# Re-ordering the first tiles and the middle matmuls of a linear-attention and routed-MLP kernel

## The chip, the cores and the metric

The kernel runs on one core of a Trainium2 chip. The metric is the device time of one execution in microseconds, the median of several runs. TensorE (PE) multiplies and writes to PSUM, which has eight banks. VectorE (DVE), ScalarE (ACT) and GpSimd (POOL) are the other engines; SyncE (SP) only issues DMAs. Each engine works through its own list of instructions in order and waits for semaphores of the others.

## The reference

With x of 2048 tokens by 640 (bf16) the result is x + A(xn) + B(x), where xn is x normalised over its 640 columns.

A is linear attention with 32 heads of 20: q, k, v = xn · wqkv; phi(t) = (t + 1 if t > 0, else exp(t)) + 1e-6; per head kv = phi(k)ᵀ v and z = sum over tokens of phi(k); the output is phi(q) · kv divided by phi(q) · z, times wo.

B takes the 8 tokens with the largest x · w_r, computes (silu(x w_gate) * (x w_up)) w_down for these, scales it by sigmoid of the score, and adds it, and x itself, to the result.

## The kernel before

The tokens form T = 16 tiles of 128, the 640 columns KC = 5 blocks of 128. The whole program is written out by hand: the order of the calls in the source is the order on each engine.

**Front and loop (L294 to L483).** For each tile t: DVE takes its statistics in two halves and joins them (`ln_stats`, L161, L164, L165); POOL turns the variance into a factor (L167, L170; for tiles 0 and 1 ACT does it, L174, L175); DVE scales the tile (`ln_scale`, L179); PE turns tiles 0 to 4 (`turn_pe`, L191), with copies out by ACT or DVE (L199, L201), and a DMA turns the rest (L204). Then come the k product (`k_mm`, L209), ACT's exp and relu of it (L225, L226), DVE's combination pk (`k_phi`, L232), and the product G of xn and pk, summed over all tiles in five PSUM banks (`g_mm`, L270). Units of the q product (`q_mm`, L243; `q_act`, L255 and L256; `q_phi`, L262) are interleaved, one for each tile. An extra column of the k weights gives the router's score; ACT stores it into r_all (L227). Loads of x are issued by SP; that of tile 3 waits for a small POOL memset (`late_x3`, L146, L147), which stands among POOL's constants. `const_piece` builds other constants on POOL during the loop.

**Middle (L486 to L780).** PE turns r_all (L487), sums pk over the tokens for z (`z_mm`, L498: four products with 32 columns each, side by side in the array, per tile), finishes G, and multiplies the 16 rows of candidates by ones to spread them over all partitions (L515). ACT copies G out of PSUM (L522, L530) and the column sums zs (L526). DVE picks the 8 tokens; POOL gathers their columns into xsT (L563). PE then interleaves: the rest of G (`grest_mm`, L279), denominators (`den_mm`, L578; `spread_mm`, L595), kv by groups of six heads (`kv_mm`, L618; five groups of 120 columns and one of 40), each group masked by DVE (L630, L638) and multiplied by wo to M (`m_mm`, L651; copied out by ACT L663 or DVE L665, and sent to its place M_sb by SP, L666), and the MLP of the 8 tokens: gate and up (`gu_mm`, L672, 32 columns, four side by side), ACT's exp, ln, exp (L724, L729, L731), two DVE products to hm (L737, L738), its turn (L741) and copy hT (L743), the down product (L748) and the add by an indirect DMA (L758).

**End.** The remaining q units, then for each tile the output product (`o_mm`, L789), DVE's add of x (L799) and the store (L806).

Of the kernel before, what the change touches and what calls it, by code (L numbers as in the profile page):

```python
# [17 lines left out]
C = 8  # L18
# [3 lines left out]
HG = 6  # L22
GB = HG * DH
NG = 6
FJ = F // 4
YW = D // 4
EPS_BF16 = 1.0013580322265625e-05
# [9 lines left out]

def group(g):

    return GB * g, min(GB, D - GB * g)  # L40


@with_exitstack
def kernel(
# [49 lines left out]
    ones_r = sb([T, P], BF16, "ones_r")  # L94
    tileoff = sb([P, T, C], F32, "tileoff")
    diag = sb([T, T], F32, "diag")
    oh8 = sb([P, C], F32, "oh8")
# [6 lines left out]
    maskkv = sb([GB, HG, DH], BF16, "maskkv")  # L104
    wr_rows = sb([KC, P], BF16, "wr_rows")
    wrT = sb([P, KC], BF16, "wrT")
    r_all = sb([P, T], BF16, "r_all")
    kvT = sb([GB, NG, GB], BF16, "kvT")
    M_nat5 = sb([GB, D], BF16, "M_nat5")
    spw = sb([P, 2, 4, 256], BF16, "spw")  # L110

# [4 lines left out]
    def psb(b):  # L116
        return ps[:, b, :].bitcast(BF16)
# [14 lines left out]
    make_identity(nc, ident[:])  # L132
    nc.gpsimd.memset(half[:, 0:1], EPS_BF16)
    nc.gpsimd.memset(half[:, 1:2], -0.5)
    nc.gpsimd.memset(gbig[:], 1.0)


# [9 lines left out]
        nc.sync.dma_start(x_sb[:, 3, :], x_v[:, 3, :])  # L147

    gbig_side(True)
    late_x3()  # L150
    gbig_side(False)

    stat = {}

# [156 lines left out]
    warm(4, P)  # L311
    turned(0, 7, "V", 0, 2)
    turned(0, 7, "A", 2, KC)
    ln_stats(2, "a")
    ln_scale(1)
    for kc in range(3):
        for h in range(2):
            k_one(0, 5, kc, h, HW)
# [43 lines left out]
    ln_scale(5)  # L362
    turn_dma(5)
    ln_stats(6)
    ln_stats(7, "a")
    k_phi(3)
    ln_scale(6)
    turn_dma(6)
    ln_stats(7, "b")
    q_mm(0, 7)  # L370
    q_act(0, 7)

    def const_piece(i):
# [22 lines left out]
            )  # L396
        elif i == 4:
            nc.gpsimd.memset(ones_r[:], 1.0)
            nc.gpsimd.memset(diag[:], 0.0)
            nc.gpsimd.affine_select(  # L400
                out=diag[:], in_=diag[:], compare_op=ALU.not_equal, fill=1.0, base=0,
                pattern=[[-1, T]], channel_multiplier=1,
            )
            nc.gpsimd.memset(oh8[:], 0.0)
            for j in range(4):
                nc.gpsimd.affine_select(
                    out=oh8[:], in_=oh8[:], compare_op=ALU.not_equal, fill=1.0,
                    base=-32 * j, pattern=[[-1, C]], channel_multiplier=1,
                )
        elif i == 5:  # L410
            nc.gpsimd.iota(itmp[:], pattern=[[1, P]], base=0, channel_multiplier=0)
            nc.gpsimd.tensor_copy(iot[:], itmp[:])
            nc.gpsimd.iota(
                itmp[:].rearrange("p (t c) -> p t c", c=C), pattern=[[P, T], [0, C]], base=0,
                channel_multiplier=0,
            )
            nc.gpsimd.tensor_copy(
                tileoff[:], itmp[:].rearrange("p (t c) -> p t c", c=C)
            )
        elif i == 6:  # L420
            nc.gpsimd.iota(itmp[:, 0:1], pattern=[[0, 1]], base=4 * S, channel_multiplier=1)
# [12 lines left out]
    def load_wo(h):  # L434
        if h == 0:
            src = A_wo[0 : 5 * GB, :].rearrange("(g e) n -> e g n", e=GB)
            nc.sync.dma_start(wo_sb[:, 0:5, :], src)
        else:
            nc.sync.dma_start(wo_sb[0 : D - 5 * GB, 5, :], A_wo[5 * GB : D, :])

    pieces += [lambda: load_wo(0), lambda: load_wo(1)]
    for kc in range(KC):
# [41 lines left out]


    u = T - 3 - 1  # L486
    nc.tensor.transpose(psb(5)[0:T, 0:P], r_all[:], ident[:])  # L487
# [21 lines left out]
    nc.vector.tensor_tensor(  # L509
        out=candm[:], in0=cand[:].unsqueeze(2).to_broadcast([T, 2, T, C]),  # L510
        in1=diag[:].unsqueeze(1).unsqueeze(3).to_broadcast([T, 2, T, C]), op=ALU.mult,
    )
    q_phi(u)
# [99 lines left out]

    def kv_mm(g0, g1, bank):
        for g in range(g0, g1):
            f0, w = group(g)
            for c in range(KC):
                nc.tensor.matmul(  # L618
                    ps[0:w, bank, (g - g0) * GB : (g - g0) * GB + w],
                    lhsT=wv_sb[:, c, f0 : f0 + w],  # L620
                    rhs=GT[:, c, f0 : f0 + w],
                    start=(g == g0 and c == 0), stop=(c == KC - 1),
                    skip_group_check=True,
                )
# [9 lines left out]
        )  # L634

    def kv_mask5(bank):
        w = group(5)[1]
        nc.vector.tensor_tensor(  # L638
            out=kvT[0:w, 5, 0:w], in0=ps[0:w, bank, GB : GB + w], in1=mask2[0:w, 0:w],
            op=ALU.mult,  # L640
        )

    late = big.tile([P, T * D], BF16, tag="pk", name="late")
# [2 lines left out]
    M_nat = big.tile([P, KC, D], BF16, tag="wk_sb", name="M_nat")  # L646

    def m_mm(g, b):
        w = group(g)[1]
        for h in range(2):  # L650
            nc.tensor.matmul(  # L651
                ps[0:w, b + h, 0:HW],
                lhsT=kvT[0:w, g, 0:w],
                rhs=wo_sb[0:w, g, h * HW : (h + 1) * HW],
                start=True, stop=True,
            )

    def m_out(g, b, by_act=False):
        f0, w = group(g)
        nat = M_nat[0:w, g, :] if g < 5 else M_nat5[0:w, :]  # L660
        dst, src = nat.rearrange("p (b f) -> p b f", b=2), ps[0:w, b : b + 2, 0:HW]
# [4 lines left out]
        nc.sync.dma_start(M_sb[f0 // KC : (f0 + w) // KC, :, :], nat)  # L666


    def gu_mm(w, b):
# [52 lines left out]
    scale_by(0, 0)  # L722
    gu_mm(wg_sb, 7)
    nc.scalar.activation(e1, ps[:, 7, 0:FJ], AF.Exp, scale=-1.0)  # L724
# [12 lines left out]
    nc.vector.tensor_tensor(out=hm, in0=ps[:, 7, 0:FJ], in1=sg, op=ALU.mult)  # L737
    nc.vector.tensor_tensor(out=hm, in0=hm, in1=ps[:, 0, 0:FJ], op=ALU.mult)  # L738
    q_unit(13, 1)
    for j in range(3):  # L740
        nc.tensor.transpose(psb(7)[:, j * P : (j + 1) * P], hm[:, j * P : (j + 1) * P], ident[:])  # L741
# [125 lines left out]
```

## Time and profile before

| | us |
|---|---|
| median of 3 runs | 111.91 (111.89 to 112.18) |
| profiled execution | 112.47 |
| its span | 110.8 |
| PE busy | 104.9 |
| DVE busy | 82.4 |
| ACT busy | 57.8 |
| POOL busy | 29.6 |

The profile is of one execution. The span runs from the first instruction to the last. A row of its timeline has start, length, engine, line, operation, what is written and read, and in brackets how long the engine was idle before and what ended that. The chain of waits follows the work that ended last back to the start; its pieces have start and length and do not overlap. PE's matmuls are pipelined: a row's length holds the time until the result is out, and the next matmul may start before that. PEld is the load of weights into the array.

### The profile page before, as it was taken

The numbers are of one execution on the slowest core, as the hardware profiler recorded it, in microseconds if no ns is written. First come the engines' busy times: TensorE is split into PE (matmuls) and PEld (weight loads), VectorE is DVE, ScalarE is ACT, GpSimd is POOL, SyncE is SP. The second block draws the span as 40 slices with busy tenths as digits, with TensorE's granted clock in tenths as the row PEclk, the third lists the DMA queues.
The fourth block names the chain that finished last, engine by engine and source line by source line (L and its number), as shares of the span: only waits on it lengthen the run. The fifth ranks groups of instructions, "written<-read, shape, count | busy, mean of one in ns | idle before, by whom it ended". The sixth has DMA issues, their size and how long they took to land.

```text
span 110.8 us, 2414 instructions
## 1 busy us (share of the span) xinstructions
PE 104.9 (95%) x881; PEld 65.0 (59%) x881; DVE 82.4 (74%) x182; ACT 57.8 (52%) x121; POOL 29.6 (27%) x83
## 2 busy tenths in 40 slices
PE   5979999999999999999999999999999999999980
PEld 2346565555556555566556578954656667777760
DVE  0767988878888898998798892586586669966680
ACT  1538746853875568555875583867599330000000
POOL 7406023537855588740000002200330000000000
PEclk9999999999999999999999999999999999999998
DMA  3999930241799999999955799415225927894333
GB/s 84 312 297 340 382 130 8 52 90 31 164 273 219 183 194 361 310 357 341 352 212 189 215 291 373 133 57 171 74 15 162 339 99 175 280 345 149 124 121 116
DMA packets 23011, 22.49 MB, mean 203 GB/s; under 512 B 8791, under 2 KB 21719, under 8 KB 22999
## 3 DMA queue, kind: packets, MB, share of 16 engines
q1 hardware_dynamic: 21021, 20.27, 63.6%
q10 hardware_dynamic: 1834, 2.02, 5.3%
q0 software_dynamic: 144, 0.04, 0.5%
q8 instruction: 7, 0.11, 0.4%
q14 instruction: 5, 0.04, 0.1%
HBM read 14.42 MB, written 5.28 MB: 178 GB/s over the span
## 4 chain that ended last, share of the span: by engine, by line
PE 77%; DVE 7%; DMA 5%; POOL 3%; issue 2%; ACT 2%; SPq 1%; DVEq 0%; POOLq 0%
PE ps L789 19%; PE ps L243 17%; PE ps L209 15%; PE ps L270 12%; DMA x_sb<-in_A_x_dram 5%; PE ps L279 4%; DVE xn L179 2%; POOL rs L170 2%; PE ps L618 2%; PE ps L651 2%; PE ps L672 2%; DVE st L164 1%; DVE xn L799 1%; PE ps L578 1%; PE ps L498 1%
## 5 line engine op out<-in xcount | busy, mean ns | idle before, releaser
L209 PE MATMUL ps<-wk_sb,xnT 128*128 128x320 bf16 (+1 forms) x160 | 25.2, 300 | 0.4 <-DVE xnT L201 0.3
L243 PE MATMUL ps<-xnT,wq_sb 128*128 128x512 bf16 x100 | 24.2, 379 | 0.0
L789 PE MATMUL ps<-late,pqT 128*128 128x320 bf16 (+2 forms) x165 | 22.3, 295 | 0.0
L209 PEld LDWEIGHTS <-xnT 128*128 128x128 bf16 x160 | 15.3, 98 | 9.2 <-DVE xnT L201 0.8
L270 PE MATMUL ps<-pk,xn 128*128 128x512 bf16 x80 | 19.9, 379 | 0.3 <-DVE pk L232 0.3
L225 ACT ACTIVATE ek<-ps 128x640 bf16<-128x640 f32 x16 | 11.3, 704 | 15.9 <-PE ps L209 15.9
L789 PEld LDWEIGHTS <-pqT 128*128 128x128 bf16 x165 | 15.8, 98 | 6.3 <-issue 0.2
L799 DVE TENSOR_TENSOR xn<-ps,x_sb 128x640 bf16<-128x640 f32 (+3 forms) x18 | 13.2, 747 | 5.5 <-PE ps L789 5.5
L262 DVE SCALAR_TENSOR_TENSOR pqT<-eq,rq 128x512 bf16<-128x512 bf16 x20 | 13.7, 684 | 3.5 <-ACT rq L256 3.5
L243 PEld LDWEIGHTS <-wq_sb 128*128 128x128 bf16 x100 | 11.5, 118 | 8.0 <-issue 0.3
L232 DVE SCALAR_TENSOR_TENSOR pk<-ek,rk 128x640 bf16<-128x640 bf16 x16 | 12.9, 804 | 1.7 <-ACT rk L226 1.7
L255 ACT ACTIVATE eq<-ps 128x512 bf16<-128x512 f32 x20 | 12.3, 617 | 2.7 <-PE ps L243 2.7
L270 PEld LDWEIGHTS <-xn 128*128 128x128 bf16 x80 | 7.6, 98 | 9.0 <-issue 0.6
L256 ACT ACTIVATE rq<-ps 128x512 bf16<-128x512 f32 x20 | 12.3, 616 | 0.0
L170 POOL TENSOR_TENSOR rs<-rs,half 128x1 f32<-128x1 f32 x14 | 11.2, 801 | 1.1
L167 POOL TENSOR_TENSOR rs<-mv,half 128x1 f32<-128x1 f32 x14 | 6.3, 447 | 18.5 <-DVE mv L165 18.5
L226 ACT ACTIVATE rk<-ps 128x640 bf16<-128x640 f32 x16 | 11.2, 700 | 0.0
L161 DVE BATCH_NORM_STATS2 st<-x_sb 128x6 f32<-128x320 bf16 x16 | 7.6, 476 | 3.9 <-DMA x_sb<-in_A_x_dram 3.9
L179 DVE TENSOR_SCALAR xn<-x_sb,mv,rs 128x640 bf16<-128x640 bf16 x16 | 7.1, 445 | 4.5 <-POOL rs L170 4.2
L164 DVE BATCH_NORM_STATS2 st<-x_sb 128x6 f32<-128x320 bf16 x16 | 7.6, 478 | 0.0
L563 POOL COPY xsT<-xnT 128x5 bf16 x8 | 1.7, 207 | 21.7 <-DVE junk L693 18.3
L185 DVE TENSOR_TENSOR x_sb<-x_sb,xn 128x640 bf16<-128x640 bf16 x16 | 6.9, 474 | 0.0
(121 smaller groups left out, 91.1 us busy)
## 6 DMA issues: line engine op xcount, KB each, us to landing
x_sb<-in_A_x_dram SPq DMA_DIRECT2D x6, 320.0 KB, 7.4
wg_sb<-in_B_w_gate_dram SPq DMA_DIRECT2D x5, 384.0 KB, 4.3
wu_sb<-in_B_w_up_dram SPq DMA_DIRECT2D x5, 384.0 KB, 5.1
wd_sb<-in_B_w_down_dram SPq DMA_DIRECT2D x3, 640.0 KB, 7.7
xxd<-x_sb SPq DMA_DIRECT2D x2, 640.0 KB
out_dram<-xn SPq DMA_DIRECT2D x8, 160.0 KB, 1.8
x_sb<-xxd SPq DMA_DIRECT2D x2, 640.0 KB, 4.9
out_dram<-xn ACTq DMA_DIRECT2D x7, 160.0 KB, 3.3
```

Source lines behind the costliest of these rows:

```text
L170: nc.gpsimd.tensor_tensor(out=rs[:, 1:2], in0=rs[:, 0:1], in1=half[:, 1:2], op=ALU.pow)
L209: nc.tensor.matmul(ps[:, b + h, 0:w], lhsT=xnT[:, kc, t * P : (t + 1) * P], rhs=wk_sb[:, kc, h * HW : h * HW + w], start=(kc == 0), stop=( ...
L225: nc.scalar.activation(e[:], ps[:, b : b + 2, 0:HW], AF.Exp)
L226: nc.scalar.activation(r[:], ps[:, b : b + 2, 0:HW], AF.Relu)
L232: nc.vector.scalar_tensor_tensor(out=pk[:, t, :].rearrange("p (b f) -> p b f", b=2), in0=e[:], scalar=1.0, in1=r[:], op0=ALU.min, op1=ALU.add,
L243: nc.tensor.matmul(ps[:, b, :], lhsT=wq_sb[:, kc, :].rearrange("p (f m) -> p m f", m=KC)[:, m, :], rhs=xnT[:, kc, tb * TBLK : (tb + 1) * T ...
L255: nc.scalar.activation(e[:], ps[:, b, :], AF.Exp)
L256: nc.scalar.activation(r[:], ps[:, b, :], AF.Relu)
L262: nc.vector.scalar_tensor_tensor(out=pqT[:, m, tb * TBLK : (tb + 1) * TBLK], in0=e[:], scalar=1.0, in1=r[:], op0=ALU.min, op1=ALU.add,)
L270: nc.tensor.matmul(ps[:, c, :], lhsT=xn[:, t, c * P : (c + 1) * P], rhs=pk[:, t, 0:512], start=(t == 0), stop=(t == T - 1),)
L789: nc.tensor.matmul(ps[:, b, 0 : c1 - c0], lhsT=pqT[:, kc, t * P : (t + 1) * P], rhs=M_sb[:, kc, c0:c1], start=(kc == 0), stop=(kc == KC - 1),)
L799: nc.vector.tensor_tensor(out=xn[:, t, c0:c1].rearrange("p (b f) -> p b f", f=w), in0=ps[:, b : b + n, 0:w], in1=x_sb[:, t, c0:c1].rearran ...
```

## The change

**Front.** DVE scales tile 1 ahead of the first half of tile 2's statistics. Tile 7's statistics are taken in one piece, ahead of tile 3's pk. POOL clears r_all ahead of its constants, and the memset that releases the load of tile 3 comes behind both selections of gbig instead of between them.

On DVE, first tiles 1 and 2 (st, mv, rs and the digit: statistics, their aggregate and the factor of that tile). Before:

```order
L201 COPY xnT_77<-ps_109 128x2x128
L161 BN_STATS st2_184<-x_sb_75 128x6
L179 TENSOR_SCALAR xn_76<-x_sb_75,mv1_158,rs1_159 128x640
L164 BN_STATS st2_184<-x_sb_75 128x6
L165 BN_AGGR mv2_185<-st2_184 128x2
```

Now:

```order
L205 COPY xnT_77<-ps_110 128x2x128
L183 TENSOR_SCALAR xn_76<-x_sb_75,mv1_160,rs1_161 128x640
L165 BN_STATS st2_187<-x_sb_75 128x6
L168 BN_STATS st2_187<-x_sb_75 128x6
L169 BN_AGGR mv2_188<-st2_187 128x2
```

Tile 1's scaling has moved up by one place. Then, on DVE, tiles 6 and 7. Before:

```order
L165 BN_AGGR mv6_335<-st6_334 128x2
L161 BN_STATS st7_342<-x_sb_75 128x6
L232 SCALAR_TENSOR_TENSOR pk_79<-ek3_327,rk3_328 128x640
L179 TENSOR_SCALAR xn_76<-x_sb_75,mv6_335,rs6_336 128x640
L164 BN_STATS st7_342<-x_sb_75 128x6
L165 BN_AGGR mv7_343<-st7_342 128x2
L262 SCALAR_TENSOR_TENSOR pqT_78<-eq0_358,rq0_359 128x512
L179 TENSOR_SCALAR xn_76<-x_sb_75,mv7_343,rs7_344 128x640
```

Now:

```order
L169 BN_AGGR mv6_337<-st6_336 128x2
L165 BN_STATS st7_344<-x_sb_75 128x6
L168 BN_STATS st7_344<-x_sb_75 128x6
L169 BN_AGGR mv7_345<-st7_344 128x2
L236 SCALAR_TENSOR_TENSOR pk_79<-ek3_329,rk3_330 128x640
L183 TENSOR_SCALAR xn_76<-x_sb_75,mv6_337,rs6_338 128x640
L266 SCALAR_TENSOR_TENSOR pqT_78<-eq0_360,rq0_361 128x512
L183 TENSOR_SCALAR xn_76<-x_sb_75,mv7_345,rs7_346 128x640
```

The second half and the aggregate of tile 7 have moved ahead of tile 3's pk and tile 6's scaling.

**Middle.** The column sums of tile 15 join the run of the others; ACT copies zs ahead of G. r_all has 128 columns, candm and ones_r 128 rows (the added ones are zero), so that both products use the whole array. The last kv group takes the last 120 columns: its product has 120 rows, its 80 columns that group 4 has already are zero in kvT, and only its last 40 rows of M are sent. The up product follows the gate product at once, then kv groups 4 and 5, q unit 13, M's groups 4 and 5, the turn of hm, and three matmuls of q unit 14 where there were two. `scale_by(0, 2)` comes after q unit 13's phi.

On PE, around the last kv groups and M. Before, between the gate products and the last three matmuls of q unit 13, with the up products in the place of the dots:

```order
L618 MATMUL ps<-GT,wv_sb 40x40
L672 LDWEIGHTS xsT
L672 MATMUL ps<-wu_sb,xsT 32x384
...
L651 MATMUL ps<-wo_sb,kvT 120x320
L651 LDWEIGHTS kvT
L651 MATMUL ps<-wo_sb,kvT 40x320
...
L243 LDWEIGHTS wq_sb
L243 MATMUL ps<-xnT,wq_sb 128x512
```

Now, with the rest of the last kv group and of q unit 13 in the place of the dots:

```order
L672 MATMUL ps<-wu_sb,xsT 32x384
L620 LDWEIGHTS wv_sb
L620 MATMUL ps<-GT,wv_sb 120x120
...
L620 MATMUL ps<-GT,wv_sb 120x40
L247 LDWEIGHTS wq_sb
L247 MATMUL ps<-xnT,wq_sb 128x512
...
L651 LDWEIGHTS kvT
L651 MATMUL ps<-wo_sb,kvT 120x320
L740 LDWEIGHTS late
L740 MATMUL ps<-ident,late 128x128
```

The up products have gone ahead of the kv groups, M's two groups behind q unit 13, and no output of 40 rows is left. The diff, cut to its core:

```diff
+W0 = NG * GB - D
 def group(g):
-    return GB * g, min(GB, D - GB * g)
+    return min(GB * g, D - GB)
...
-    r_all = sb([P, T], BF16, "r_all")
+    r_all = sb([P, P], BF16, "r_all")
...
+    nc.gpsimd.memset(r_all[:], 0.0)
     nc.gpsimd.memset(gbig[:], 1.0)
...
     gbig_side(True)
+    gbig_side(False)
     late_x3()
-    gbig_side(False)
...
+    ln_scale(1)
     ln_stats(2, "a")
-    ln_scale(1)
...
     ln_stats(6)
-    ln_stats(7, "a")
+    ln_stats(7)
     k_phi(3)
     ln_scale(6)
     turn_dma(6)
-    ln_stats(7, "b")
...
             nc.gpsimd.memset(ones_r[:], 1.0)
+            nc.gpsimd.memset(candm[:], 0.0)
+            nc.gpsimd.memset(kvT[:, NG - 1, 0 : W0], 0.0)
...
-            nc.sync.dma_start(wo_sb[0 : D - 5 * GB, 5, :], A_wo[5 * GB : D, :])
+            nc.sync.dma_start(wo_sb[:, 5, :], A_wo[D - GB : D, :])
...
-    nc.tensor.transpose(psb(5)[0:T, 0:P], r_all[:], ident[:])
+    nc.tensor.transpose(psb(5)[:, 0:P], r_all[:], ident[:])
...
-    for t in range(T - 1):
+    for t in range(T):
         z_mm(t)
...
     g_mm(T - 1, 3, KC)
-    z_mm(T - 1)
-    for c in range(4):
-        nc.scalar.copy(GT[:, c, 0:512], ps[:, c, :])
...
-    nc.scalar.copy(GT[:, 4, 0:512], ps[:, 4, :])
+    for c in range(KC):
+        nc.scalar.copy(GT[:, c, 0:512], ps[:, c, :])
...
-            f0, w = group(g)
+            f0, c0 = group(g), (W0 if g == NG - 1 else 0)
             for c in range(KC):
                 nc.tensor.matmul(
-                    ps[0:w, bank, (g - g0) * GB : (g - g0) * GB + w],
-                    lhsT=wv_sb[:, c, f0 : f0 + w],
-                    rhs=GT[:, c, f0 : f0 + w],
+                    ps[0:GB, bank, (g - g0) * GB : (g - g0 + 1) * GB - c0],
+                    lhsT=wv_sb[:, c, f0 : f0 + GB],
+                    rhs=GT[:, c, f0 + c0 : f0 + GB],
...
     nc.scalar.activation(e1, ps[:, 7, 0:FJ], AF.Exp, scale=-1.0)
+    gu_mm(wu_sb, 0)
     kv_mm(4, 6, 6)
     scale_by(0, 1)
+    nc.scalar.activation(e1, e1, AF.Ln, bias=1.0)
+    nc.scalar.activation(sg, e1, AF.Exp, scale=-1.0)
     kv_mask(4, 5, 6)
     kv_mask5(6)
-    nc.scalar.activation(e1, e1, AF.Ln, bias=1.0)
-    gu_mm(wu_sb, 0)
-    nc.scalar.activation(sg, e1, AF.Exp, scale=-1.0)
+    nc.vector.tensor_tensor(out=hm, in0=ps[:, 7, 0:FJ], in1=sg, op=ALU.mult)
+    nc.vector.tensor_tensor(out=hm, in0=hm, in1=ps[:, 0, 0:FJ], op=ALU.mult)
+    q_unit(13, 1)
     m_mm(4, 2)
     m_out(4, 2, True)
     m_mm(5, 4)
     m_out(5, 4, True)
-    scale_by(0, 2)
-    nc.vector.tensor_tensor(out=hm, in0=ps[:, 7, 0:FJ], in1=sg, op=ALU.mult)
-    nc.vector.tensor_tensor(out=hm, in0=hm, in1=ps[:, 0, 0:FJ], op=ALU.mult)
-    q_unit(13, 1)
...
-    q_mm(14, 6, 0, 2)
+    q_mm(14, 6, 0, 3)
...
     q_phi(13)
+    scale_by(0, 2)
...
-    q_mm(14, 6, 2)
+    q_mm(14, 6, 3)
```

More of the change, by code (lines that the diff above doesn't have):

```diff
@@ L93 @@
     ones_bf = sb([P, H], BF16, "ones_bf")
-    ones_r = sb([T, P], BF16, "ones_r")
+    ones_r = sb([P, P], BF16, "ones_r")
     tileoff = sb([P, T, C], F32, "tileoff")
@@ L106 @@
     wrT = sb([P, KC], BF16, "wrT")
-    r_all = sb([P, T], BF16, "r_all")
+    r_all = sb([P, P], BF16, "r_all")
     kvT = sb([GB, NG, GB], BF16, "kvT")
+    candm = sb([P, 2, T, C], BF16, "candm")
     M_nat5 = sb([GB, D], BF16, "M_nat5")
@@ L490 @@
     idxu = sb([T, C], U32, "idxu")
-    candm = sb([T, 2, T, C], BF16, "candm")
     nc.vector.tensor_copy(rT[:], psb(5)[0:T, 0:P])
@@ L509 @@
     nc.vector.tensor_tensor(
-        out=candm[:], in0=cand[:].unsqueeze(2).to_broadcast([T, 2, T, C]),
+        out=candm[0:T], in0=cand[:].unsqueeze(2).to_broadcast([T, 2, T, C]),
         in1=diag[:].unsqueeze(1).unsqueeze(3).to_broadcast([T, 2, T, C]), op=ALU.mult,
@@ L636, in kv_mask5 @@
     def kv_mask5(bank):
-        w = group(5)[1]
         nc.vector.tensor_tensor(
-            out=kvT[0:w, 5, 0:w], in0=ps[0:w, bank, GB : GB + w], in1=mask2[0:w, 0:w],
-            op=ALU.mult,
+            out=kvT[:, NG - 1, W0:GB], in0=ps[0:GB, bank, GB : 2 * GB - W0],
+            in1=mask2[:, W0:GB], op=ALU.mult,
         )
@@ L648, in m_mm @@
     def m_mm(g, b):
-        w = group(g)[1]
         for h in range(2):
             nc.tensor.matmul(
-                ps[0:w, b + h, 0:HW],
-                lhsT=kvT[0:w, g, 0:w],
-                rhs=wo_sb[0:w, g, h * HW : (h + 1) * HW],
+                ps[0:GB, b + h, 0:HW],
+                lhsT=kvT[:, g, :],
+                rhs=wo_sb[:, g, h * HW : (h + 1) * HW],
                 start=True, stop=True,
@@ L658, in m_out @@
     def m_out(g, b, by_act=False):
-        f0, w = group(g)
-        nat = M_nat[0:w, g, :] if g < 5 else M_nat5[0:w, :]
-        dst, src = nat.rearrange("p (b f) -> p b f", b=2), ps[0:w, b : b + 2, 0:HW]
+        f0, r0 = group(g), (W0 if g == NG - 1 else 0)
+        nat = M_nat[0:GB, g, :] if g < 5 else M_nat5[:]
+        dst, src = nat.rearrange("p (b f) -> p b f", b=2), ps[0:GB, b : b + 2, 0:HW]
         if by_act:
@@ L665, in m_out @@
             nc.vector.tensor_copy(dst, src)
-        nc.sync.dma_start(M_sb[f0 // KC : (f0 + w) // KC, :, :], nat)
+        nc.sync.dma_start(M_sb[(f0 + r0) // KC : (f0 + GB) // KC, :, :], nat[r0:GB, :])
     def gu_mm(w, b):
```

## The prediction

> **What bounds the kernel now.** I read the page first (engine shares, the chain that ended last), then the chain in order of time, then the timeline of the two places where the chain leaves TensorE.
>
> ```profile
> 25.07:61.60 36.53, 36.53 (x205) 20.95 (x204) 31.64 (x67) 24.04 (x52) 16.71 (x47) 1.00 0.91 241
> ```
>
> This row is of a view by windows: length, busy time of PE, weight loads, DVE, ACT and POOL, granted clock, DMA. From 25.07 on PE is never idle, at a granted clock of 1.00. So the time is a front up to 25 us in which PE waits for others, and behind it a stream of matmuls whose own length counts. Each microsecond taken from a PE wait in the front, or from the stream, comes off the end; what other engines do matters only where it makes PE wait. The profiled execution took 112.47 us (1.7 of it around its span) and lies 0.56 us above the median of the runs (111.91). I make the sum against 112.47 and take the same difference off the median.
>
> In the front PE waits long twice. The first wait, in the timeline (start, length, engine):
>
> ```profile
> 6.24 1.18 PE L209 MATMUL ps<-wk_sb,xnT 128*128 128x320 bf16 x6 [0.16 <-DVE xnT L201]
> 6.35 0.20 ACT L175 ACTIVATE rs<-rs 128x1 f32<-128x1 f32 x1
> 6.99 0.49 DVE L161 BATCH_NORM_STATS2 st<-x_sb 128x6 f32<-128x320 bf16 x1 [0.80 <-DMA x_sb<-in_A_x_dram]
> 7.88 0.45 PE L191 MATMUL ps<-ident,xn 128*128 128x128 bf16 x5 [0.46 <-DVE xn L179]
> 8.39 0.45 DVE L161 BATCH_NORM_STATS2 st<-x_sb 128x6 f32<-128x320 bf16 x1
> 9.43 0.45 DVE L179 TENSOR_SCALAR xn<-x_sb,mv,rs 128x640 bf16<-128x640 bf16 x1
> ```
>
> Tile 1's factor was ready at 6.55 (6.35 + 0.20), but DVE had the statistics of tile 2 ahead of tile 1's scaling and stood 0.80 us for the load of tile 2. PE waited for that scaling until 7.88. The second wait:
>
> ```profile
> 19.24 0.81 DVE L232 SCALAR_TENSOR_TENSOR pk<-ek,rk 128x640 bf16<-128x640 bf16 x1
> 19.38 1.07 POOL L170 TENSOR_TENSOR rs<-rs,half 128x1 f32<-128x1 f32 x1
> 20.49 0.45 DVE L179 TENSOR_SCALAR xn<-x_sb,mv,rs 128x640 bf16<-128x640 bf16 x1 [0.44 <-POOL rs L170]
> 21.02 1.24 PE L270 MATMUL ps<-pk,xn 128*128 128x512 bf16 x5
> 22.26 0.55 POOL L170 TENSOR_TENSOR rs<-rs,half 128x1 f32<-128x1 f32 x1
> 22.84 0.45 DVE L179 TENSOR_SCALAR xn<-x_sb,mv,rs 128x640 bf16<-128x640 bf16 x1 [0.71 <-POOL rs L170]
> 23.49 1.24 PE L243 MATMUL ps<-xnT,wq_sb 128*128 128x512 bf16 x5
> 24.24 0.77 DVE L232 SCALAR_TENSOR_TENSOR pk<-ek,rk 128x640 bf16<-128x640 bf16 x1
> 25.07 1.24 PE L270 MATMUL ps<-pk,xn 128*128 128x512 bf16 x5 [0.34 <-DVE pk L232]
> ```
>
> DVE stands twice for POOL's factor (0.44 and 0.71), so tile 4's pk comes late. Five matmuls of 512 columns take 1.08 each time in the chain (below), 0.216 apiece; PE's five from 23.49 leave it free at 24.57, and it starts at 25.07: 0.50 us are lost.
>
> **The change in the front.** Scaling tile 1 ahead of the statistics of tile 2: it can start at about 6.59 (0.04 behind its factor) and end at 7.03, PE could turn tile 1 near 7.1. PE itself is busy with the six matmuls until about 7.26 (its last start, 1.18 − 0.31 behind 6.24, plus 0.14), so the turn moves from 7.88 to 7.26. Of these 0.62 us not all stays. Tile 2's statistics cannot start before its load (6.99), but their second half no longer stands behind a scaling of 0.45, which holds the next one up by some 0.36. So tile 2's scaling moves from 9.43 to about 9.07, and PE, 0.62 earlier by its own work, is held by it. All later steps of the front hang on this one by fixed links: **−0.36 us**. The bounds: 0 if tile 3's statistics, which stand between, hold DVE, and −0.45 if the whole scaling counts.
>
> Statistics of tile 7 in one piece: the second half (0.4) and the aggregate (0.2) fill the time in which DVE stood 0.44 for POOL. In the time scale of before, tile 3's pk starts at 19.92 instead of 19.24 and ends at 20.73, 0.29 before PE wants it (21.02); tile 6's scaling slips by about 0.17. But POOL gets tile 7's variance 1.6 us earlier. How fast it answers is open. One side: 0.55, as at 22.26, gives its factor near 21.2. Other side: POOL stands behind every DVE instruction with two inputs, as in the 1.07 at 19.38, and finishes only when DVE falls idle, near 22.3. Tile 7's scaling then starts between 21.7 and 22.4 instead of 22.84, tile 4's pk is done between 23.9 and 24.6, and PE asks at 24.57. Both ends cover the wait: **−0.50 us** (bounds −0.45 and −0.50). The three memsets that POOL gets in the loop (464 columns, at most the 0.61 of a selection over 512 that is shown under rival d) lie ahead of factors of tiles that PE needs three rounds of the loop later; that covers them, and without the cover they would cost those 0.6.
>
> **The change in the stream.** The chain of waits counts PE's groups end to end, so a row's length is what the group adds:
>
> ```profile
> 60.65 1.08 PE ps L270 x5
> 61.73 0.15 PE ps L487
> 61.88 1.04 PE ps L498 x60
> 62.92 0.75 PE ps L270 x3
> 63.67 0.21 PE ps L515
> 63.88 0.54 PE ps L270 x2
> 64.42 0.18 PE ps L498 x4
> 64.60 2.12 PE ps L279 x36
> 67.38 1.24 PE ps L618 x20
> 70.51 0.82 PE ps L651 x6
> ```
>
> Three matmuls of L270 cost 0.75 behind the column sums (three clean ones 0.65), two behind the 16-row product 0.54 (clean 0.43), four column sums 0.18 where four in the run cost 0.07 (1.04 / 15). So a change between the whole array (128*128) and a part of it (32 or 16 columns, 16 rows) costs about 0.1 on each side. The 120-wide groups L618 and L651 follow and precede 128-wide ones at 0.062 and 0.137 apiece, without it: 120 counts as whole. Before, these seven rows from L487 make 4.99. After: transposing r_all with 128 columns is like one of L279 (0.06); 64 column sums behind a change 0.18 + 15 × 0.07 = 1.23 (before, the narrow transpose took that change); L270 x3 0.75; the product of 256 columns with 128 rows half of 0.216, 0.11; L270 x2 0.43; L279 x36 without a change 2.02. Sum 4.60: **−0.39 us**. Bounds: −0.30 (10% of the run more), −0.45. ACT makes the same six copies of zs and G, zs first; PE's next reader of either stands behind L279 x36, whose 2.02 covers that.
>
> ```profile
> 72.49 0.93 PE ps L672 x20
> 73.42 0.64 PE ps L618 x10
> 74.06 0.93 PE ps L672 x20
> 74.99 0.79 PE ps L651 x4
> 75.77 1.21 PE ps L243 x5
> 76.98 0.17 PE ps L741 x3
> 77.15 0.43 PE ps L243 x2
> 77.60 1.01 PE ps L748 x48
> ```
>
> Gate and up together: the second twenty lose their entry, 0.93 to about 0.85 (−0.08). L618: five of its ten were narrow; with 120 columns the change inside goes (−0.1), but their pace is not in the trace: 0.025 as narrow ones (0.64 less two changes and five wide ones), or 0.062 as wide ones. I take the middle, −0.02, bounds −0.10 and +0.08. L651 x4 held two changes: 4 × 0.137 = 0.55 (−0.24). L243 behind no change 1.08 (−0.13). PE waited for hT ahead of L748 (1.01 against 12 × 0.07 + 0.10 = 0.94, and a gap of 0.02); a third matmul of q unit 14 now runs there (−0.09). Sum −0.56.
>
> Against it stands the product hm, which PE now wants sooner:
>
> ```profile
> 71.82 0.21 POOL L563 COPY xsT<-xnT 128x5 bf16 x1 [0.49 <-issue]
> 73.47 0.49 ACT L724 ACTIVATE late<-ps 128x384 f32<-128x384 f32 x1 [0.25 <-PE ps L672]
> 75.77 0.55 DVE L738 TENSOR_TENSOR late<-late,ps 128x384 bf16<-128x384 bf16 x1
> ```
>
> From the end of the gate products, 73.42, to hm, 76.32, it takes 2.90, and the three ACT steps in it keep their length. PE now has 0.85 + 0.62 + 1.08 + 0.55 = 3.10 of work for that time, less the 0.16 by which starts lead ends; hm's two steps also stand behind the masks of the later L618. So PE comes at about +2.85 and hm at +3.0: a new wait of 0.15 (bounds 0 and 0.35). **Net −0.41 us.** The last gathered column, 72.03, was 0.4 ahead of PE and is now level with it; I cost that at 0 (bound 0.1). Queued behind ACT's q unit 13 now are the copies of M's groups 4 and 5 and SP's transfers of them, about 1 us later; their reader, the output product, starts behind L748 and 27 more matmuls of L243 (27 × 0.216 = 5.8 us), which hides that; without them it would be that 1 us. The 100 KB more of wo are asked for in the loop, dozens of microseconds ahead of use.
>
> Sum: −0.36 − 0.50 − 0.39 − 0.41 = −1.66, so 112.47 → 110.81, and the median 111.91 → 110.25. I say **110.2 us**.
>
> [...] The trace's load of 120 columns is long beside the pace:
>
> ```profile
> L618 PEld LDWEIGHTS <-wv_sb 128*120 128x120 bf16 x25 | 1.5, 134 | 0.5 <-issue 0.3 <-DMA wd_sb<-in_B_w_down_dram 0.2
> ```
>
> It takes 134 ns, yet these matmuls follow each other at 62 ns (1.24 / 20): loads overlap. [...]
>
> **Rivals.** (a) *The weights set the pace of the 40-column products*: each lasts at most its load, 5 × (0.134 − 0.043) = 0.45 over my middle: 110.7. For it: so few columns hide no load. Against: 62 ns at 120 columns. [...] (b) *PE waits for data in the new places*: the gate chain and the gather take the whole second gain and 0.1 more, −1.15: 110.8. For it: both are level with PE. Against: each is short of slack by tenths only. (c) *POOL's factors stay late*: DVE now runs without a pause there, POOL never gets in, and PE's 0.50 remains: 110.75. Against: DVE must pause for that very factor. (d) *The load of tile 3 comes late*; this one ends slower:
>
> ```profile
> 3.12 0.33 SPq L147 DMA_DIRECT2D x_sb<-in_A_x_dram  x1
> 3.12 0.61 POOL L140 TENSOR_SCALAR_AFFINE_SELECT gbig<-gbig 128x512 bf16<-128x512 bf16 x1
> ```
>
> Its issue waits for POOL, which now runs one selection (0.61) and a memset more first, so some 0.8 to 1.0 later. Its statistics stand in DVE's order ahead of tile 2's scaling; they began at 8.39 without a wait, so it had landed, and I want them at 8.05. Landing d behind 8.05 shifts everything by d: with the old 8.39 plus 1.0 the result is 111.6, at the edge of no change; from 10.1 on (7.0 us behind the old issue) the kernel is slower by over 0.3%, and at 10.5 it takes 112.7. For it: DVE did stand 0.80 for the load of tile 2, so loads queue. Against: tile 3, asked for at 3.12, was not awaited at all.
>
> **Chances.** Forecast 0.60; (a) 0.07, (b) 0.12, (c) 0.10, (d) slower 0.04, (d) in part or two of these together, ending between 110.9 and 111.7, 0.07. About 0.3%, 0.34 us, is what a measurement of this kernel can tell from no change. Of the last case 0.05 falls within it: faster 0.91, same 0.05, slower 0.04. The forecast's own bounds: −0.45 − 0.50 − 0.45 − 0.64 gives 109.9, and −0.25 − 0.45 − 0.30 − 0.20 gives 110.7; (a) to (c) reach 110.8, and a part of (d) 111.1. Range 109.9 to 111.1.
>
> **What would show it.** Right: PE's turn of tile 1 near 7.3, of tile 2 near 9.6; no wait at the first L270 behind 23 us; one group of 64 column sums near 1.23; one of 40 gate and up products near 1.78; L651 x4 near 0.55; a short wait ahead of the turning of hm. Wrong: DVE waiting for tile 3's load, PE for xsT, or the 40-column products above 0.1 apiece.

## The result, and the profile after

The changed kernel takes 110.81 us in the median (110.76 to 111.10), beside 112.04 for the kernel before (111.89 to 112.42) on the same chip: a ratio of 0.9891, 95% interval 0.9873 to 0.9909. Two more comparisons gave 110.78 beside 112.22 (0.9873, 0.9851 to 0.9895) and 110.80 beside 112.18 (0.9874, 0.9853 to 0.9896). So the change brings 1.2 to 1.4 us. The profiled execution took 110.76 us, its span is 109.0. The prediction's sum against its own execution, 112.47 − 1.66 = 110.81, is what came; the number it gave, 110.2, is 0.6 too low. The measured 110.81 lies in the stated range, but just outside the band of the forecast itself (109.9 to 110.7), and the rivals (a) to (c) stood at 110.7 to 110.8. So the number alone does not tell the forecast from them; the rows below do. The ratios leave out executions in a slower state, of which three occur below: 276.79 of the kernel before, 113.48 and 113.44 with tile 2 loaded earlier.

The front in the timeline of the changed kernel (start, length, engine; L165 and L168 are the halves of the statistics, L169 their aggregate, L183 the scaling, L195 PE's turn; the instructions between these are left out, here and in the timelines below):

```profile
6.39 0.20 ACT L179 ACTIVATE rs<-rs 128x1 f32<-128x1 f32 x1
6.63 0.45 DVE L183 TENSOR_SCALAR xn<-x_sb,mv,rs 128x640 bf16<-128x640 bf16 x1 [0.40 <-ACT rs L179]
6.99 0.49 DVE L165 BATCH_NORM_STATS2 st<-x_sb 128x6 f32<-128x320 bf16 x1
7.30 0.44 PE L195 MATMUL ps<-ident,xn 128*128 128x128 bf16 x5
8.03 0.45 DVE L165 BATCH_NORM_STATS2 st<-x_sb 128x6 f32<-128x320 bf16 x1
9.08 0.45 DVE L183 TENSOR_SCALAR xn<-x_sb,mv,rs 128x640 bf16<-128x640 bf16 x1
9.58 0.45 PE L195 MATMUL ps<-ident,xn 128*128 128x128 bf16 x5
```

DVE scales tile 1 0.04 behind its factor, and PE turns it at 7.30 (7.88 before), tile 2 at 9.58 (9.96 before). Tile 2's statistics begin at 6.99, as before, but now right behind the scaling, without a wait. Tile 3's (8.03) name no load. The second place, tiles 6 and 7:

```profile
19.67 0.66 POOL L171 TENSOR_TENSOR rs<-mv,half 128x1 f32<-128x1 f32 x1
20.40 0.64 POOL L174 TENSOR_TENSOR rs<-rs,half 128x1 f32<-128x1 f32 x1
21.15 0.44 DVE L183 TENSOR_SCALAR xn<-x_sb,mv,rs 128x640 bf16<-128x640 bf16 x1
22.55 0.77 DVE L236 SCALAR_TENSOR_TENSOR pk<-ek,rk 128x640 bf16<-128x640 bf16 x1
23.12 1.24 PE L247 MATMUL ps<-xnT,wq_sb 128*128 128x512 bf16 x5
24.20 1.24 PE L274 MATMUL ps<-pk,xn 128*128 128x512 bf16 x5
```

POOL has tile 7's factor at 21.04, DVE scales it at 21.15 (22.84 before), and tile 4's pk is done at 23.32 (22.55 + 0.77). PE comes from its five matmuls to the product of tile 4 at 24.20 without a pause: five times 0.216 behind 23.12. From the turn of tile 2 to this product it takes 14.62 us, 15.11 before.

The middle, in the chain of waits (start, length, what ran):

```profile
60.86 0.06 PE ps L492
60.92 1.22 PE ps L502 x64
62.14 0.16 issue
62.30 0.59 PE ps L274 x2
62.89 0.11 PE ps L519
63.00 0.43 PE ps L274 x2
63.43 2.01 PE ps L283 x36
...
71.25 1.74 PE ps L672 x40
72.99 0.66 PE ps L620 x10
73.65 0.06 issue
73.71 1.02 PE ps L247 x4
74.73 0.55 PE ps L651 x4
75.28 0.25 PE ps L740 x3
75.52 0.65 PE ps L247 x3
76.17 0.94 PE ps L748 x48
...
77.29 5.78 PE ps L247 x26
```

The trace lacks eight of the 881 matmuls; a missing one stands as a piece of "issue" (0.16 and one matmul of L274 too few, for example). The seven rows from r_all's turn to L283 take 4.58 us from start to end, 4.99 before. From the gate products on, to the output product, it is 11.82 (71.25 to 83.07), against 12.29 before (72.49 to 84.78).

So in the two profiles the prediction's terms stand thus:

| Term | predicted | from the two profiles |
|---|---|---|
| tile 1 scaled first (start of tile 2's turn) | −0.36 | 9.96 → 9.58: −0.38 |
| tile 7's statistics in one piece (from that turn to tile 4's product) | −0.50 | 15.11 → 14.62: −0.49 |
| column sums and whole-array products | −0.39 | 4.99 → 4.58: −0.41 |
| gate and up, last group, hT, less the wait for hm | −0.41 | 12.29 → 11.82: −0.47 |

Each agrees to 0.06. The stretch between the second and the third place takes 0.04 more (65.44 to 71.25, 5.81, against 5.77 before), and with it the four make −1.71, which is all of 112.47 → 110.76. Yet in the medians 0.2 to 0.4 us of the forecast is missing. The experiments ask where.

### The profile page after: what moved, and what is told of

The parts are those of the page before. It is cut to its first block, busy times and chain, and to the rows that moved or that the text cites. A ratio compares the mean times of both kernels' runs of the same rounds, so it can differ in the third digit from the quotient of the medians.

```text
span 109.0 us, 2409 instructions
## 1 busy us (share of the span) xinstructions
PE 103.2 (95%) x873; PEld 65.5 (60%) x881; DVE 82.6 (76%) x182; ACT 57.8 (53%) x121; POOL 30.0 (27%) x86
## 3 DMA queue, kind: packets, MB, share of 16 engines
q10 hardware_dynamic: 1834, 2.02, 5.3%
## 4 chain that ended last, share of the span: by engine, by line
PE 86%; DVE 6%; DMA 3%; issue 1%; ACT 0%; SPq 0%; DVEq 0%
PE ps L247 20%; PE ps L789 19%; PE ps L213 18%; PE ps L274 16%; PE ps L283 4%; DMA x_sb<-in_A_x_dram 3%; PE ps L620 2%; PE ps L672 2%; PE ps L651 2%; DVE xn L799 1%; DVE st L165 1%; PE ps L580 1%; DVE xn L183 1%; PE ps L502 1%; DVE st L168 1%
## 5 line engine op out<-in xcount | busy, mean ns | idle before, releaser
L247 PE MATMUL ps<-xnT,wq_sb 128*128 128x512 bf16 x95 | 23.6, 379 | 0.4 <-issue 0.2
L274 PE MATMUL ps<-pk,xn 128*128 128x512 bf16 x77 | 19.3, 379 | 0.3 <-issue 0.2
L266 DVE SCALAR_TENSOR_TENSOR pqT<-eq,rq 128x512 bf16<-128x512 bf16 x20 | 13.8, 688 | 2.9 <-ACT rq L260 2.8
L274 PEld LDWEIGHTS <-xn 128*128 128x128 bf16 x80 | 7.7, 98 | 8.4
L174 POOL TENSOR_TENSOR rs<-rs,half 128x1 f32<-128x1 f32 x14 | 10.6, 760 | 1.1
L165 DVE BATCH_NORM_STATS2 st<-x_sb 128x6 f32<-128x320 bf16 x16 | 7.7, 478 | 3.3 <-DMA x_sb<-in_A_x_dram 3.3
L183 DVE TENSOR_SCALAR xn<-x_sb,mv,rs 128x640 bf16<-128x640 bf16 x16 | 7.2, 451 | 3.7 <-POOL rs L174 3.3
L168 DVE BATCH_NORM_STATS2 st<-x_sb 128x6 f32<-128x320 bf16 x16 | 7.6, 476 | 0.0
```

The lines of the kernel that those rows point to most:

```text
L174: nc.gpsimd.tensor_tensor(out=rs[:, 1:2], in0=rs[:, 0:1], in1=half[:, 1:2], op=ALU.pow)
L247: nc.tensor.matmul(ps[:, b, :], lhsT=wq_sb[:, kc, :].rearrange("p (f m) -> p m f", m=KC)[:, m, :], rhs=xnT[:, kc, tb * TBLK : (tb + 1) * T ...
L266: nc.vector.scalar_tensor_tensor(out=pqT[:, m, tb * TBLK : (tb + 1) * TBLK], in0=e[:], scalar=1.0, in1=r[:], op0=ALU.min, op1=ALU.add,)
L274: nc.tensor.matmul(ps[:, c, :], lhsT=xn[:, t, c * P : (c + 1) * P], rhs=pk[:, t, 0:512], start=(t == 0), stop=(t == T - 1),)
```

## The experiments

My theory after the result: the term of tile 1 counts a surplus that this one execution of the kernel before had (it took 112.47, the medians are 112.0 to 112.3), and the other terms are real. The rival: every term is fixed, and something outside these places gives part back.

**The two kernels again, and the halves of the change.** First both kernels unchanged:

> The kernel before, unchanged, for a second profile. Theory 1 (the profiled execution of before was a long one: 112.47 against a median of 112.04, and the surplus of 0.4 lies in the front, where PE hangs on the load of tile 2): the time is 111.9 to 112.1, the span 110.3 to 110.4, and in the profile PE turns tile 2 at about 9.5 instead of 9.96, everything behind being as it was. Theory 2 (the front is the same in every execution, the surplus is in the matmul stream or in the granted clock): PE turns tile 2 at 9.96 again and the surplus is found behind 25 us.

The kernel before again: 112.16 us, ratio 0.9997 (0.9981 to 1.0013). The profiled execution took 112.32; its front:

```profile
6.40 0.29 DVE L201 COPY xnT<-ps 128x256 bf16<-128x256 bf16 x1 [0.33 <-PE ps L191]
6.83 0.49 DVE L161 BATCH_NORM_STATS2 st<-x_sb 128x6 f32<-128x320 bf16 x1
9.81 0.44 PE L191 MATMUL ps<-ident,xn 128*128 128x128 bf16 x5
```

The same program turned tile 2 at 9.81 here and at 9.96 in the execution that the prediction was read from, and was 0.15 us shorter: neither the 9.5 of the first theory nor the 9.96 of the second. DVE names no load here, and its copy had waited for PE. But tile 2's statistics start 0.43 behind the start of that copy, where an execution shown below needs 0.21 (6.40 to 6.61). The other 0.22 are probably the load again; no row says so.

112.47 is not a rare time for this kernel. Of the 65 executions of it in all these comparisons (without that of 276.79), 18 took 112.40 or more and 23 took 112.10 or less; their median is 112.18.

> The changed kernel, unchanged. Both theories: 110.8, ratio 0.989, and a span of 109.1; theory 1 expects the front to agree within 0.1 us with the first profile of it, since PE no longer hangs on the load of tile 2 there.

The changed kernel again: 110.78, and tile 2 is turned at 9.62 (9.58 in the first).

Then the three edits of the front alone:

```diff
     gbig_side(True)
-    late_x3()
     gbig_side(False)
+    late_x3()
...
-    ln_stats(2, "a")
     ln_scale(1)
+    ln_stats(2, "a")
...
-    ln_stats(7, "a")
+    ln_stats(7)
     k_phi(3)
...
-    ln_stats(7, "b")
```

> Before with the three front edits alone (scaling of tile 1 first, statistics of tile 7 in one piece, load of tile 3 released later). The forecast's terms: -0.86 against a long execution like the first profiled one. Theory 1: against the median only -0.86 + 0.4 = about -0.45 (111.55). Theory 2: -0.86 (111.15).

111.66 us (111.63 to 111.70), ratio 0.9955 (0.9938 to 0.9971): −0.56 in the medians, where the two terms make −0.86. And the changed kernel with these three edits undone:

> After with the three front edits undone, so the matmul edits alone. The forecast's terms: -0.39 - 0.41 = -0.80, by theory 1 in every execution (111.2). Theory 2: the surplus is in the stream, so about -0.4 (111.6).

111.34 (111.31 to 111.39), ratio 0.9926 (0.9909 to 0.9942): −0.88 where the two terms make −0.80. The wait ahead of tile 4's product is back, with the same late scaling of tile 7 ahead of it:

```profile
22.61 0.45 DVE L183 TENSOR_SCALAR xn<-x_sb,mv,rs 128x640 bf16<-128x640 bf16 x1 [0.71 <-POOL rs L174]
24.84 1.02 PE L274 MATMUL ps<-pk,xn 128*128 128x512 bf16 x4 [0.35 <-DVE pk L236]
```

The halves add up: −0.56 − 0.88 = −1.44, and the whole change measured −1.44 beside them. To the hundredth that is luck, since each of the three is uncertain by about 0.2. Within that, nothing is given back elsewhere, and what is missing is missing in the front.

**Each of the front's edits alone.** The first two edits, without that of tile 7:

```diff
     gbig_side(True)
-    late_x3()
     gbig_side(False)
+    late_x3()
...
-    ln_stats(2, "a")
     ln_scale(1)
+    ln_stats(2, "a")
```

> Only tile 1's scaling goes ahead of tile 2's statistics (and the load of tile 3 behind the second gate constant); the rest is the kernel before. Theory 1, the term of the prediction (a fixed 0.36 us): about 112.3 - 0.36 = 111.9, a ratio near 0.997. Theory 2 (the 0.36 us was the surplus of one long execution; where tile 2 is there when the front copies are done, the old order starts the turn of tile 2 at 9.65 to 9.8, the new one at 9.6): 0 to 0.15 us, a ratio of 0.9985 to 1.000. Under both the profile has the turn of tile 2 at 9.55 to 9.65.

112.22 us beside 112.18: ratio 1.0000 (0.9985 to 1.0015). The fixed −0.36 (0.9968) lies outside. Tile 2 was turned at 9.68, a little later than both theories had it:

```profile
8.57 1.27 PE L209 MATMUL ps<-wk_sb,xnT 128*128 128x320 bf16 x8
9.68 0.44 PE L191 MATMUL ps<-ident,xn 128*128 128x128 bf16 x5
```

DVE had tile 2 scaled by 9.53, as in the changed kernel, but PE came to it only behind its own eight matmuls.

Then tile 7's edit without those two:

```diff
-    ln_stats(7, "a")
+    ln_stats(7)
     k_phi(3)
...
-    ln_stats(7, "b")
```

> Only the statistics of tile 7 in one piece, ahead of tile 6's scaling. Both theories: 0.45 to 0.5 us less than the kernel before, a ratio near 0.9957; from the turn of tile 2 to the products with wo 74.2 us instead of 74.66, and no wait of TensorE near 25 us for the sums of tile 7. If it is worth clearly more (0.56 or above), the front's gain measured with all three edits was all this edit's and scaling tile 1 first is worth nothing.

111.65, ratio 0.9947 (0.9927 to 0.9967): −0.53 in the medians, about all that the front's three edits gave together. The turn of tile 2 came at 9.92 in its profiled execution, tile 4's product at 24.52, 14.60 later, without a wait. It holds one row that the prediction would not have expected of the old order:

```profile
8.31 0.49 DVE L161 BATCH_NORM_STATS2 st<-x_sb 128x6 f32<-128x320 bf16 x1 [0.22 <-DMA x_sb<-in_A_x_dram]
```

Here tile 3's load, asked for early as before, was awaited for 0.22 us.

**Tile 1's scaling put back in the changed kernel**, behind the first half of tile 2's statistics, twice, the second time beside the changed kernel itself:

```diff
+    ln_stats(2, "a")
     ln_scale(1)
-    ln_stats(2, "a")
```

> After with one edit undone: the first half of tile 2's statistics again ahead of tile 1's scaling. Theory of the load (scaling first is worth only as much as tile 2's load is late; in three profiles with the old order DVE began these statistics at 6.99, 6.83 and 6.74, and PE turned tile 2 at 9.96, 9.81 and 9.72, against 9.58 to 9.62 with scaling first): the median is 110.8 to 110.95, no more than 0.15 above the changed kernel, with a spread of 0.4 or more between executions. Theory of the fixed term (the edit takes 0.36 off every execution, as forecast): 111.15, spread as before.

110.71 us (110.55 to 111.15), ratio 0.9863 (0.9840 to 0.9886): below even the 110.8 to 110.95 that was expected, with the spread that was expected.

> The changed kernel as it is, to stand beside the next run on the same chip: 110.7 to 110.9, ratio 0.986 to 0.989. Theory 1: 0.3 to 0.4 us less than the next run. Theory 2: within 0.1 us of it.

> The changed kernel with the first half of tile 2's statistics ahead of tile 1's scaling again. Theory 1: 111.1 to 111.2, 0.3 to 0.4 us above the run before. Theory 2: within 0.1 us of it. In the profile the start of the turn of tile 0's products tells whether TensorE was still at 107 ns a matmul then; at that pace the copy of the turned tile 0 ends at about 6.7 and tile 2's statistics cannot be what DVE waits for, at 56 ns it ends at 6.2 and they can.

On one chip: 110.80 (110.76 to 110.86) for the changed kernel, 0.9874 (0.9853 to 0.9896); 110.58 (110.57 to 110.76) with the scaling put back, 0.9862 (0.9837 to 0.9887). Both theories missed: one wanted 0.3 to 0.4 more, the other the same within 0.1, and it is 0.2 less. Putting it back costs nothing; whether it gains those 0.2 is open, since the intervals overlap. The profiles tell why it costs nothing. First the one of the second time:

```profile
5.48 0.45 PE L195 MATMUL ps<-ident,xn 128*128 128x128 bf16 x5 [0.28 <-DVE xn L183]
6.17 0.48 DVE L165 BATCH_NORM_STATS2 st<-x_sb 128x6 f32<-128x320 bf16 x1
9.40 0.44 PE L195 MATMUL ps<-ident,xn 128*128 128x128 bf16 x5
```

Tile 2 is there at 6.17, its statistics fill the time in which DVE in the new order waits 0.40 for tile 1's factor, and PE turns tile 2 at 9.40: earlier than in any profiled execution of the new order. The first time had this instead:

```profile
5.63 0.74 PE L195 MATMUL ps<-ident,xn 128*128 128x128 bf16 x5
6.40 0.29 DVE L205 COPY xnT<-ps 128x256 bf16<-128x256 bf16 x1 [0.33 <-PE ps L195]
6.61 0.48 DVE L165 BATCH_NORM_STATS2 st<-x_sb 128x6 f32<-128x320 bf16 x1
9.65 0.44 PE L195 MATMUL ps<-ident,xn 128*128 128x128 bf16 x5
```

PE worked at half the pace (0.74 for the five; the next matmuls start at 6.16, so one each 0.106 us, where the first profile of the changed kernel has 0.056), so DVE's copy and all behind it came 0.4 later, and the turn 0.25. In the changed kernel the half pace costs almost nothing, as its third profile shows:

```profile
5.63 0.69 PE L195 MATMUL ps<-ident,xn 128*128 128x128 bf16 x5
6.63 0.45 DVE L183 TENSOR_SCALAR xn<-x_sb,mv,rs 128x640 bf16<-128x640 bf16 x1
9.61 0.44 PE L195 MATMUL ps<-ident,xn 128*128 128x128 bf16 x5
```

There DVE starts the scaling at 6.63 with the factor, whatever PE did, and the tile is turned at 9.61 where the first profile had 9.58. PE's own work leaves no more room than that: in the run with the first two edits alone, where the half pace lasted longer (0.74 for the five), the turn came at 9.68, as shown above.

Put side by side (turn of tile 2; span, to two digits as the trace has it, and time of that same execution; the part of the span behind the turn):

| Kernel | order of tile 2's statistics | turn of tile 2 | span | time | span − turn |
|---|---|---|---|---|---|
| before | old | 9.96 | 110.76 | 112.47 | 100.80 |
| before, again | old | 9.81 | 110.61 | 112.32 | 100.80 |
| first two edits alone | new | 9.68 | 110.48 | 112.20 | 100.80 |
| tile 7's edit alone | old | 9.92 | 110.21 | 112.01 | 100.29 |
| front's three edits | new | 9.58 | 109.89 | 111.69 | 100.31 |
| front's edits undone | old | 9.72 | 109.67 | 111.39 | 99.95 |
| after, first | new | 9.58 | 109.05 | 110.76 | 99.47 |
| after, second | new | 9.62 | 109.10 | 110.81 | 99.48 |
| after, third | new | 9.61 | 109.06 | 110.77 | 99.45 |
| after, scaling put back, first | old | 9.65 | 109.10 | 110.82 | 99.45 |
| after, scaling put back, second | old | 9.40 | 108.87 | 110.58 | 99.47 |

Executions that differ in the first tiles alone have the same span behind the turn, to within 0.03 us. Tile 7's edit takes 0.51 off it, the middle 0.85, and both together 1.33 (100.80 to 99.47). So what lies behind the turn of tile 2 is fixed, and the forecast's three other terms, −1.30, are there in full. What lies outside the span is 1.71 or 1.72, and 1.80 in the two kernels that have tile 7's edit with the old middle; why is not known.

What lies ahead of the turn varies: it comes between 9.40 and 9.96 in the profiled executions of the old order, between 9.58 and 9.68 in those of the new one. In the old order it always follows 2.06 to 2.08 behind the turn of tile 1, by PE's own work, and what varies is the turn of tile 1 (7.34 to 7.88). That hung on the load of tile 2 in the first profile (0.80), on PE's half pace in others (0.74 for the five turning matmuls, beside 0.45), and in tile 7's run also on the k weights, for which PE waited 0.29. In the new order tile 1 is turned from 7.30 on, but DVE has tile 2 scaled at 9.53 at the earliest, so the turn of tile 2 comes at 9.58 or later. The new order cuts off the late turns, and the early ones too.

The times agree, as far as they go: 13 of 16 executions of the changed kernel lie between 110.76 and 110.86, the others at 110.61, 111.07 and 111.10, while those of before spread from 111.88 to 112.71. But the six with the front's edits undone, in the old order, lie within 0.08 (111.31 to 111.39), so the old order need not scatter. The median of before, 112.04 to 112.33 in these comparisons, corresponds to a turn at 9.53 to 9.82 (an estimate: that median less 102.51, which is 112.47 − 9.96), about where the new order has it. That the median execution has its turn there is inferred; the profiles of before are of 112.32 and 112.47.

The later release of tile 3's load was run together with tile 1's scaling and not by itself, so the 0.00 belongs to the pair.

**Tile 2 loaded earlier.** If the old order is quicker once tile 2 is there early, its load could be asked for ahead of the k weights, on ScalarE's queue: once in the changed kernel, once with tile 1's scaling put back as well.

```diff
+    nc.scalar.dma_start(x_sb[:, 2, :], x_v[:, 2, :])
     nc.scalar.dma_start(wk_sb[:, 0:3, 0:D], ...
...
-    nc.sync.dma_start(x_sb[:, 2, :], x_v[:, 2, :])
```

> After, with tile 2 loaded from ACT's queue ahead of the k weights instead of from SP's behind tile 1. Theory of the load: with scaling first DVE cannot use the earlier load, PE turns tile 2 at about 9.6 as it does, 110.75 to 110.85; the k weights come up to 0.5 later, which PE has just room for. Theory of the fixed term: 110.8 as well.

111.71 us, ratio 0.9911 (0.9880 to 0.9942), against 110.75 to 110.85 expected: a miss. Six of the seven executions, all but that of 113.48, range from 110.81 to 111.76, with a median of 111.45.

> Both: tile 2 loaded early and its statistics ahead of tile 1's scaling. Theory of the load: DVE does the first half while it waits for tile 1's factor (6.2 to 6.6), tile 2's chain starts 0.4 earlier, PE turns tile 2 at 9.2 to 9.4: 110.4 to 110.6, so scaling first costs here 0.2 to 0.4. Theory of the fixed term: the old order costs 0.36 as always, 111.15.

111.43, ratio 0.9909 (0.9882 to 0.9936), against 110.4 to 110.6 expected: a miss too. Five of the six executions, all but that of 113.44, range from 110.81 to 111.59. The timeline of one that took 111.50:

```profile
6.55 0.48 DVE L165 BATCH_NORM_STATS2 st<-x_sb 128x6 f32<-128x320 bf16 x1
7.46 0.98 PE L213 MATMUL ps<-wk_sb,xnT 128*128 128x320 bf16 x6 [0.93 <-DMA wk_sb<-in_A_wqkv_dram]
8.36 0.21 ACT L324 COPY wk_sb<-wrT 128x5 bf16<-128x5 bf16 x1 [1.22 <-DMA wk_sb<-in_A_wqkv_dram]
8.81 0.49 DVE L165 BATCH_NORM_STATS2 st<-x_sb 128x6 f32<-128x320 bf16 x1 [0.78 <-DMA x_sb<-in_A_x_dram]
10.35 0.44 PE L195 MATMUL ps<-ident,xn 128*128 128x128 bf16 x5
```

Tile 2 was there, but the k weights came 0.93 to 1.22 late for PE and ACT, and tile 3 0.78 late for DVE. What the one load gains the others lose in this execution: the turn comes at 10.35, and 99.44 us of span lie behind it, as in the changed kernel.

**The last kv group of 40 again**, all else as changed (its core):

```diff
-    return min(GB * g, D - GB)
+    return GB * g, min(GB, D - GB * g)
...
-                    lhsT=wv_sb[:, c, f0 : f0 + GB],
+                    lhsT=wv_sb[:, c, f0 : f0 + w],
...
-                lhsT=kvT[:, g, :],
-                rhs=wo_sb[:, g, h * HW : (h + 1) * HW],
+                lhsT=kvT[0:w, g, 0:w],
+                rhs=wo_sb[0:w, g, h * HW : (h + 1) * HW],
```

> After, with the last kv group of 40 columns again (its products, mask, M and transfers as before), all else as in after. Theory that a product of part of the array costs 0.1 at each change: the ten L618 about 0.64 to 0.70 with a change inside, M's four about 0.79 instead of 0.55, a change to the turn of hm, together 0.25 to 0.4 more on PE up to that turn; part of it may go into the short wait for hm. Rival (40 columns cost as much as 120, the gain of that stretch came from the order alone): M's four at 0.55 to 0.6.

One execution: 111.01 us. The chain of waits:

```profile
71.26 1.74 PE ps L671 x40
73.00 0.64 PE ps L617 x10
73.64 1.21 PE ps L245 x5
74.84 0.65 PE ps L650 x4
75.49 0.27 PE ps L739 x3
75.77 0.65 PE ps L245 x3
```

It starts 0.01 later than the changed kernel and reaches the three matmuls of q unit 14 at 75.77 instead of 75.52: the narrow group costs 0.24. It sits behind the narrow matmuls: 1.21 for q unit 13's five, where the changed kernel has 0.06 + 1.02, 0.65 for the four of M where it has 0.55, and 0.27 for the turn of hm where it has 0.25, less 0.02 for the ten of kv themselves (0.64 beside 0.66). The span behind the turn of tile 2 agrees: 99.71, against 99.45 to 99.48. M's four were expected at 0.79 and took 0.65; the rest of the expected surplus stands in the rows ahead of and behind them. So part of the array costs about 0.1 at each change, as the prediction had it, and the 0.24 are just under the 0.25 to 0.4 expected.

## Why the prediction was right and wrong

**The step that failed** is the one that joins the sum to the median: "I make the sum against 112.47 and take the same difference off the median", and with it the size of the first term, −0.36. The mechanism was read rightly: in that execution DVE did stand for tile 2's load, and the new order takes the wait away (9.96 → 9.58). But 112.47 was among the longer executions of the kernel before, and it was long at that very place. The term repairs what the median execution mostly doesn't have: alone it measures 0.00 us (−0.17 to +0.17). The quoted row, 0.80 us for a DMA, was not a fixed duration: in the second profile of the same kernel that row has no such wait. The 0.56 us between the quoted execution and the median had to come from something that varies, and the same term was then taken off a median that held little of it. With 0 in its place the sum against the medians is −1.30, and −1.23, −1.44 and −1.38 were measured.

The prediction had the better value at hand. It gives 0 as a bound of this term, but the forecast's band of 109.9 to 110.7 is added up with −0.25; likewise the bounds of the fourth term leave −0.11, where −0.20 went in. With the stated bounds the band would have ended at about 111.05, and 110.81 lies in it.

That 112.47 less the sum, 110.81, was met to the hundredth is in part luck. Most executions of the changed kernel lie close together, so its profile and its median nearly agree; but the single terms missed by up to 0.06 and made up for each other.

**Tile 7's statistics in one piece**: right. −0.50 predicted, −0.49 between the profiles, −0.51 behind the turn and −0.53 (−0.82 to −0.37) in the medians alone. POOL answered on the early side of the two bounds, 0.64 and 0.66 per step; it did not stand behind every DVE instruction with two inputs, as the late side had it, but was done at 21.04, ahead of the end of DVE's L266 at 21.24 (20.55 + 0.69). Tile 7's scaling, at 21.15, even came ahead of the 21.7 that was the earliest in the prediction, and the end of the wait is PE's own work, as said.

**The stream**: −0.80 predicted for the two terms, −0.84 in the rows that end to end lead from 60.86 to 83.07 (22.21, 23.05 before), −0.88 (−0.65 to −1.02) in the medians. Within it: 64 column sums 1.22 (1.23 predicted), 256 columns by 128 rows 0.11 (0.11), L283 2.01 (2.02), 40 gate and up products 1.74 (1.78), M's four 0.55 (0.55), L748 0.94 (0.94). Two terms were off by less than a tenth. The ten of L620 cost 0.66 (0.62 predicted): the five that stream 40 columns start mostly 0.055 apart, not the 0.043 of my middle. And the turn of hm takes 0.25 where 0.17 stood, so the wait for hm is 0.08 instead of 0.15. That was a slip in the sum: 3.10 less 0.16 is 2.94, not 2.85, and hm at +3.0 then leaves a wait of 0.06. With it the net term would have been −0.50; −0.47 came. Column sums and gate part were not run apart from each other; their split rests on the two chains.

**The rivals.** (a) Weights that set the pace would have made the five of L620 cost 0.134 apiece, a row of ten of 0.98; it is 0.66, so the loads are hidden. The trace of before has 134 ns for a load of 120 columns, as in the prediction's row, and 97 ns for one of 40:

```profile
L618 PEld LDWEIGHTS <-wv_sb 128*40 128x40 bf16 x5 | 0.2, 97 | 0.1
```

So by the trace's loads the change from 40 to 120 columns adds 37 ns to each. (b) PE waits for hm, for 0.08, and the gate products begin 5.81 behind the end of L283 (65.44 to 71.25), 5.77 before: no wait for the gathered columns to speak of. (c) is refuted by tile 7's scaling at 21.15. (d) No execution of the changed kernel shown here waited for tile 3. But the load isn't as safe as "was not awaited at all" made it: with the old, earlier issue DVE stood 0.22 for it in one execution.

## What to carry to other kernels

The wait for a load in the first microseconds, read from one profile, was a draw here, not a price. Take two profiles of the kernel before, see whether the wait and the total move together, and price the edit against the median execution. Where an edit replaces a dependence on a landing time by a dependence on a calculation, expect less scatter rather than a lower median (here 9.58 to 9.68 for the turn of tile 2, beside 9.40 to 9.96). What lies behind the first tiles could be summed here from rows of the chain to a tenth of a microsecond, since the groups of an engine that never waits stand end to end. A band should be added up from the very bounds that the terms were given.

## What the runs showed of the hardware that was not expected

TensorE's pace doubled within the first microseconds, at a place that differed between executions of the same program, and the granted clock didn't show it. In the changed kernel's first profile the matmuls of 512 columns started 0.427 us apart up to 3.91, against 0.216 from 23.12 on, and those of 128 columns 0.056 apart from 4.89 on. The five turning matmuls took 0.45 there from 5.44 on, in its third profile 0.69 from 5.63 on, 0.106 apiece up to 6.16; the four behind them took 0.39 in both, but 0.63 in the second profile of before. The row by windows of the changed kernel's third profile has a granted clock of 1.00 all the same (the columns are length, PE, weight loads, DVE, ACT, POOL, granted clock, DMA share, GB/s):

```profile
5.50:6.50 1.00, 1.00 (x13) 0.87 (x10) 0.64 (x3) 0.40 (x2) 0.00 (x0) 1.00 1.10 362
```

What sets the place is not shown by these traces.

Tile 2's load, asked for at 1.72 in the first profile of before, was there only at 6.99, and by 6.62 in the run of tile 7's edit, which asks for its first loads in the same order. It was there by 6.17 in an execution where tile 3's load was asked for later, at 3.96 instead of 3.12. Why was not tried, and stays open. That an earlier load delays others of this front is what the timeline with tile 2 loaded earlier shows: the k weights were 0.93 to 1.22 late there and tile 3 0.78.
